# Early loads, casts and PE order of a fused linear-attention and ELU feed-forward kernel, arranged anew

## The chip, the cores and the metric

The kernel runs on one core of one Trainium2 chip. A time is the device time of one execution in microseconds (us). Five engines work side by side, each through its own queue of instructions: PE (TensorE: matmuls and transposes; its weight loads are shown as PEld), DVE (VectorE), ACT (ScalarE), POOL (GpSimd) and SP (SyncE, which here only issues DMAs). POOL issues the loads of the weights and of most q, k and v.

## The reference

```
def _attn_ref(q, k, v):                 # each 8 batches x 8 heads x 576 x 64
    q_s = softmax(q, axis=-1)           # over the 64 elements of a head
    k_s = softmax(k, axis=2)            # over the 576 positions
    kv = np.einsum('bhsd,bhse->bhde', k_s, v)
    return np.einsum('bhsd,bhde->bhse', q_s, kv)

def _moe_ref(x, w_in, w_out):           # x: 4608 x 512, w_in: 512 x 2048, w_out: 2048 x 512
    h = x @ w_in
    g = np.where(h > 0.0, h, np.exp(np.minimum(h, 0.0)) - 1.0)
    return g @ w_out

def reference(...):
    x = attn_out.transpose(0, 2, 1, 3).reshape(B * S, H * D)
    return _moe_ref(x, w_in, w_out)
```

The two softmax calls stand here for the lines that subtract the maximum, take the exponential and divide by the sum.

## The kernel before, in words

**Attention.** The work is cut into 16 units (`n`), two for each batch. For a unit, ACT takes the exponentials of q and k (L395 or, in two parts, L419; L399), DVE sums q over the head (L421), inverts (L423), and DVE or POOL multiplies (L433, the result is `QS`). Units 0 and 1 do q in two parts of 5 and 4 chunks. `v` is cast to bf16 (`VB`, a copy by `copy`, L277). PE transposes `QS` (L457, copied out as `qsT`), forms k^T v (L507), DVE divides it by the sums of k into `MBLK` (L516, L520), and PE multiplies `qsT` with `MBLK` (L550 for the first two units, L538 later). The result is copied (L277) into `XT`, which holds x transposed.

**Feed-forward.** The 4608 tokens are 9 blocks of 512 (`j`). For each block there are 8 groups (`g`) of 256 columns of d_ff. A group is 8 matmuls of 512 columns of `XT` with `W1` (L620, in `hg_mm`), then ELU: exp on ACT (L646), and either ACT's relu (L648) with DVE's L652, or DVE's L657 and L659. The result is `GR`. For blocks 0 and 1 the second product with `W2` is direct (L673, in `out_mm`): 4 token slices by 16 row tiles `jj`, 64 matmuls for a block. From block 2 on it goes in pairs of blocks with sums of halves (L733, L757, L806).

**Block 0 is special.** The products of its groups 0 to 2 with `W1` go by `kc`, the four quarters of d_model, as units 0 and 1 and W1's quarters arrive; groups 3 to 7 come whole, in the order 3, 4, 5, 7, 6. The second product of block 0 goes by quarters of `W2` (`jj` 0 to 3, 4 to 7, 8 to 11, 12 to 15), and among its matmuls stand the transposes, k^T v and L538 of units 2 and 3, which block 1 needs.

**Loads.** SP issues q, k and v of units 0 and 1. POOL issues everything else that the first 50 us need, in this order: W1 for groups 0 to 2 in four pieces by `kc` (384 KB each, the first held back until k0 has landed), W1 for groups 3, 4 and 5 (512 KB each), W1 for groups 6 and 7 (1 MB), and then the quarters of W2 (1 MB each) and q, k, v of units 2 and 3 (576 KB each). `load_w1` (L377), `load_w2` (L385) and `load` (L359) record these.

**Order.** Each operation is recorded by `S.add` with the engines that may do it, its cost, and what it reads and writes; it gets a number. The strings of `ORDER` give each engine's numbers in a fixed order (found beforehand by a solver), and which engine does an operation that several could do follows from the string that it stands in. `AFTER` holds extra pairs (a waits for b). Spare matmuls (L892) fill PE until the first real work. `emit` issues the instructions with their semaphores.

Of the kernel before, what the change touches and what calls it, by code (L numbers as in the profile page):

```python
# [11 lines left out]
B, H, S, D = 8, 8, 576, 64  # L12
# [37 lines left out]
    "act": (  # L50
# [12 lines left out]
    "dve": (  # L63
# [37 lines left out]
}  # L101

AFTER = ((208, 196), (227, 255), (234, 268), (300, 281))


class Op:
    __slots__ = ("eng", "dur", "emit", "deps", "key", "idx", "start", "end",
                 "dma", "sem", "val", "clock", "nbytes", "side", "early", "alts")

# [165 lines left out]
class Gen:  # L275
# [586 lines left out]
    def program(self):  # L862
# [4 lines left out]
        for n, t in ((0, "q"), (1, "q"), (0, "k"), (0, "v"), (1, "k"), (1, "v")):  # L867
            self.load(n, t, -40, "sp")
            if (n, t) == (0, "k"):
                gate = S.ops[-1]  # L870
# [219 lines left out]
```

## Time and profile before

| | us |
|---|---|
| median of 3 runs | 291.89 |
| lowest and highest run | 291.81, 292.03 |
| profiled execution: span from its first to its last instruction | 290.4 |
| PE busy | 280.6 (97%) |
| DVE, ACT, POOL busy | 225.5, 209.7, 167.8 |
| first matmul with W1 (L620) | 14.20 |
| first matmul with W2 (L673) | 29.68 |
| first matmul of block 1 with W1 | 48.28 |
| first matmul of block 2 with W1 | 70.94 |

The profile is of one execution and gives its span, counted from the first to the last instruction; the runs are timed from outside, and the profile holds no outside time of that execution itself. The median is 1.5 us above the span. Times of rows are counted from the start of the span. A row of the timeline merges neighbouring instructions of one kind: its start, its length, and xcount of them.

### The profile page before, as it was taken

How to read it: one execution, taken by the hardware profiler on the slowest of the kernel's cores; microseconds unless marked ns; L12 is line 12 of the kernel's file. 1: busy time of each engine (PE TensorE's matmuls, PEld its weight loads, DVE VectorE, ACT ScalarE, POOL GpSimd, SP SyncE). 2: the span in 40 equal slices, each digit the busy share in tenths (PEclk: the TensorE clock that was granted, in tenths of full speed). 3: DMA queues.
4: the chain of work that ended last, by engine and by line, in shares of the span. 5: the costliest groups of instructions: out<-in, count | busy, mean ns of one | idle time of the engine just before them, and what ended most of it. 6: DMA issues, size and time to landing. Idle time of an engine off the chain costs nothing.

```text
span 290.4 us, 5465 instructions
## 1 busy us (share of the span) xinstructions
PE 280.6 (97%) x2176; PEld 243.7 (84%) x2176; DVE 225.5 (78%) x425; ACT 209.7 (72%) x237; POOL 167.8 (58%) x161
## 2 busy tenths in 40 slices
PE   2899999999999999999999999999999999999995
PEld 0488787778888899989999988989999999988995
DVE  3758834777699978989996987688977786794884
ACT  4857839989899899968995598975385656665510
POOL 1991335523869778676574886757314234277741
PEclk9999999999999999999999999999999999999999
DMA  7999999798896838739939295313102002300334
GB/s 259 399 363 390 389 389 339 163 260 323 238 349 163 241 91 228 202 78 305 178 96 222 56 292 129 76 40 71 46 18 56 0 2 67 78 2 1 92 73 128
DMA packets 36474, 50.04 MB, mean 172 GB/s; under 512 B 16352, under 2 KB 18144, under 8 KB 36448
## 3 DMA queue, kind: packets, MB, share of 16 engines
q1 hardware_dynamic: 29680, 33.96, 43.7%
q0 software_dynamic: 6528, 15.47, 17.8%
q8 instruction: 17, 0.28, 0.5%
q10 hardware_dynamic: 240, 0.26, 0.3%
q14 instruction: 9, 0.07, 0.1%
HBM read 36.70 MB, written 9.44 MB: 159 GB/s over the span
## 4 chain that ended last, share of the span: by engine, by line
PE 94%; DMA 2%; POOL 2%; SPq 0%; issue 0%; DVE 0%
PE PS L620 46%; PE PS L806 32%; PE PS L673 10%; PE PS L538 3%; DMA KR<-in_k_dram 2%; PE PS L507 2%; POOL W L377 1%; POOL VB L277 0%; PE PS L457 0%; POOL QS L433 0%; SPq L359 0%; PE PS L550 0%; DVE OSB L815 0%
## 5 line engine op out<-in xcount | busy, mean ns | idle before, releaser
L620 PE MATMUL PS<-XT,W 128*128 128x512 f32 x576 | 142.0, 393 | 0.1
L620 PEld LDWEIGHTS PS<-XT,W 128*128 128x128 f32 x576 | 105.0, 188 | 21.2 <-DVE GR L659 0.5
L652 DVE SCALAR_TENSOR_TENSOR GR<-PS,GE 128x512 fp32r<-128x512 f32 x112 | 76.8, 686 | 18.7 <-ACT GE L648 16.7
L646 ACT ACTIVATE GE<-PS 128x1024 f32<-128x1024 f32 x56 | 57.4, 1025 | 40.0 <-PE PS L620 34.2
L757 POOL TENSOR_TENSOR GR<-GR 128x256 fp32r<-128x256 f32 (+1 forms) x48 | 47.2, 996 | 31.5 <-DVE SB L757 16.6
L648 ACT ACTIVATE GE<-GE 128x1024 f32<-128x1024 f32 x56 | 59.4, 1061 | 1.4
L806 PE MATMUL PS<-W,GR 128*128 128x256 f32 x336 | 53.7, 283 | 0.0
L806 PE MATMUL PS<-TB,GR 128*128 128x256 f32 x336 | 51.3, 283 | 0.0
L806 PEld LDWEIGHTS PS<-W,GR 128*128 128x128 f32 x336 | 47.6, 191 | 1.7
L806 PEld LDWEIGHTS PS<-TB,GR 128*128 128x128 f32 x336 | 45.7, 191 | 0.7
L433 POOL TENSOR_TENSOR QS<-QR,RZQ 128x1152 f16<-128x1152 f32 (+1 forms) x16 | 30.4, 1898 | 21.4 <-DVE RZQ L423 19.7
L815 DVE TENSOR_TENSOR OSB<-OSB,PS 128x256 f32<-128x256 f32 x84 | 34.7, 416 | 10.3 <-PE PS L806 9.2
L673 PE MATMUL PS<-W,GR 128*128 128x512 f32 x128 | 32.7, 396 | 0.0
L757 POOL TENSOR_TENSOR GR<-SB,GR 128x256 fp32r<-128x256 f32 (+1 forms) x18 | 17.3, 971 | 24.6 <-PE PS L806 12.7
L673 PEld LDWEIGHTS PS<-W,GR 128*128 128x128 f32 x128 | 23.3, 188 | 5.0 <-DMA W<-in_moe_w_out_dram 0.5
L757 POOL TENSOR_TENSOR SB<-GR 128x256 fp32r<-128x256 f32 (+1 forms) x20 | 19.2, 965 | 13.7 <-DVE GR L652 6.4
L421 DVE TENSOR_REDUCE ZQ<-QR 128x18 f32<-128x1152 f32 (+2 forms) x18 | 21.7, 1207 | 6.1 <-ACT QR L419 4.8
L757 DVE TENSOR_TENSOR GR<-GR 128x256 fp32r<-128x256 f32 (+1 forms) x36 | 21.3, 603 | 0.6 <-PE PS L806 0.6
L277 POOL CAST VB<-VR 128x1152 bf16<-128x1152 f32 (+1 forms) x11 | 11.9, 1084 | 13.1 <-DMA VR<-in_v_dram 13.1
L646 ACT ACTIVATE ESB<-PS 128x1024 f32<-128x1024 f32 x16 | 16.1, 1024 | 4.5 <-PE PS L620 3.4
L399 ACT ACTIVATE KR<-KR 128x1152 bf16<-128x1152 f32 x16 | 18.4, 1155 | 0.8 <-DMA KR<-in_k_dram 0.8
L277 ACT ACTIVATE XT<-PS 128x512 fp32r<-128x512 f32 (+6 forms) x23 | 13.6, 595 | 6.3 <-PE PS L538 3.2
(58 smaller groups left out, 271.4 us busy)
## 6 DMA issues: line engine op xcount, KB each, us to landing
out_dram<-OSB SPq DMA_DIRECT2D x61, 128.0 KB, 2.4
QR<-in_q_dram SPq DMA_DIRECT2D x12, 576.0 KB, 4.9
KR<-in_k_dram SPq DMA_DIRECT2D x12, 576.0 KB, 6.3
VR<-in_v_dram SPq DMA_DIRECT2D x12, 576.0 KB, 5.1
W<-in_moe_w_out_dram POOLq DMA_DIRECT2D x4, 1024.0 KB, 16.7
QR<-in_q_dram POOLq DMA_DIRECT2D x4, 576.0 KB, 12.1
VR<-in_v_dram POOLq DMA_DIRECT2D x4, 576.0 KB, 13.0
KR<-in_k_dram POOLq DMA_DIRECT2D x4, 576.0 KB, 11.1
```

Of the source, the lines that this page charges most:

```text
L277: return e.activation(dst, src, AF.Copy) if e is self.nc.scalar else e.tensor_copy(dst, src)
L399: S.add("act", t_act(1152, False), lambda e: e.activation(ek[:, :, :, :].rearrange("p h c d -> p (h c d)"), flat(k), AF.Exp), key - 2, X=[ ...
L421: S.add("dve", t_dve(m), lambda e, qp=qp, zp=zp: e.tensor_reduce(zp, qp, AX.X, ALU.add), key - 3, R=[f"qR{i}{x}" for x in xs], W=[f"ZQ{i}{ ...
L433: lambda e, qp=q[:, :, a:b, :], rz=rz, dst=qs[:, :, a:b, :]: e.tensor_tensor(dst, qp, rz, ALU.mult),
L620: last = e.matmul(P[:, t * 512:(t + 1) * 512], self.W1[:, kc, tt * 128:(tt + 1) * 128], self.XT[:, kc, rc:rc + BLK], start=(kc == 0), stop ...
L646: S.add("act", t_act(1024, True), lambda e: e.activation(ge, P, AF.Exp), key, W=own, X=banks)
L648: S.add("act", t_act(1024, False), lambda e: e.activation(ge, ge, AF.Relu, bias=1.0, scale=-1.0), key, X=own)
L652: S.add("dve", t_dve(512 if j else 1024), lambda e, u=u: e.scalar_tensor_tensor(*(x[:, :, u, :] if j else x for x in (gt, P)), 0.0, ge[:, ...
L673: last = e.matmul(dst, self.tile(jb, jj, ts), self.W2[:, jj, c0:c1], start=(jj == 0), stop=(jj == 15))
L757: lambda e: e.tensor_tensor(dst, a, b, op), key, R=R, W=W, X=X, after=after)
L806: last = e.matmul(dst, a[i][:, y_, :], b[i][:, y_, :], start=start and i == 0 and y_ == 0, stop=stop and i == len(grps) - 1 and y_ == z - ...
L815: S.add("dve", t_dve(256), lambda e: e.tensor_tensor(dst, a, b, ALU.add), key, R=R, W=W, X=X, after=after)
```

## The change

- **W1.** The three transfers for groups 3, 4 and 5 become one of 1.5 MB (rows of 3 KB in place of 1 KB). The first quarter (`kc` 0) of groups 0 to 2 comes in two pieces, group 0 (128 KB) and groups 1 and 2 (256 KB). POOL issues `kc` 3 first, then groups 1 and 2 of `kc` 0, group 0 of it, `kc` 1, `kc` 2, groups 3 to 5.
- **The gate.** These first five transfers wait for the exponential of k0 on ACT (operation 21), by five pairs in `AFTER`; before, the first waited for the landing of k0.
- **The queue after that.** q2, W1 groups 6 and 7, W2's first and second quarter, v2, k2, q3, W2's third quarter, k3, v3, and W2's last quarter in two halves of 512 KB. Before: W1 groups 6 and 7, W2's first quarter, q2, the second quarter, q3, v2, k2, the third and the last quarter, k3, v3.
- **The product with W2's last quarter** (block 0) goes in pieces of two matmuls in place of four.
- **Engines.** The `VB` casts of units 0 and 1 (640 and 512 elements each) go to DVE (before: ACT 640, POOL 512). The products L433 of units 0, 2 and 3 swap: POOL takes the 5 chunks, DVE the 4; unit 1's are both on DVE. Unit 2's cast goes from POOL to ACT, the copy of its transposes from ACT to DVE. Of block 0's four output copies, DVE does two in place of none. Unit 3's transposes and L538 use the PSUM tile `AB` in place of `C`.
- **PE's order.** The 13 spare matmuls (13 rather than 12, in groups of 8, 1, 3, 1) stand elsewhere; among the L673 pieces the side work of units 2 and 3 stands at other places (unit 3's k^T v ahead of the whole last quarter, its two L538 with one piece or more between them); the two halves of block 1's group 1 stand ahead of the last two pieces of block 0's second product. From about 75 us on, all orders are the same but for the numbers, which are 4 higher.

```diff
@@ ORDER, first rows
     "pe": (
-        "35 52 33 37 56 57 54 60 80 78 79 64 65 82 81 84 87 85 88 83 86 89 99 103 110 133 121 107 "
-        "147 148 155 156 149 125 150 158 157 127 153 168 145 171 169 151 176 175 170 177 159 178 "
-        "172 165 192 194 191 193 253 259 258 257 265 211 264 266 272 220 270 271 277 279 283 222 "
+        "34 32 51 36 53 55 59 56 79 78 63 64 81 82 84 87 85 88 80 83 86 89 99 103 110 133 121 107 "
+        "148 147 156 155 125 149 157 127 150 158 145 168 151 170 153 171 169 159 177 175 178 165 "
+        "176 179 172 180 196 198 181 182 195 197 257 263 261 268 262 269 215 270 276 275 274 281 "
...
     "gp": (
-        "1 32 14 15 24 16 17 18 48 40 19 20 21 69 68 70 73 72 71 74 75 76 77 120 131 116 143 163 "
+        "1 27 18 15 14 16 17 19 67 20 68 69 71 70 72 73 74 75 76 77 119 131 142 139 163 144 132 "
...
-AFTER = ((208, 196), (227, 255), (234, 268), (300, 281))
+AFTER = ((212, 200), (231, 259), (238, 272), (304, 285), (14, 21), (15, 21), (16, 21), (17, 21), (18, 21))
...
-    def load_w2(self, s, key, after=()):
+    def load_w2(self, jj0, jj1, key):
         w = self.w_out.rearrange("(jj p) c -> p jj c", p=128)
-        sl = slice(s * 4, (s + 1) * 4)
+        sl = slice(jj0, jj1)
         self.S.add("gp", ISSUE["gp"], lambda e: e.dma_start(self.W2[:, sl, :], w[:, sl, :]), key,
-                   W=[f"W2_{s}"], dma=f"w2{s}", nbytes=1 << 20, after=after)
+                   W=[f"W2_{s}" for s in range(jj0 // 2, jj1 // 2)], dma=f"w2{jj0}", nbytes=jj1 - jj0 << 18)
...
-            if (n, t) == (0, "k"):
-                gate = S.ops[-1]
-        self.load_w1(0, 3, (0,), -30, [gate])
+        self.load_w1(0, 1, (0,), -30)
+        self.load_w1(1, 3, (0,), -30)
         for kc in range(1, 4):
             self.load_w1(0, 3, (kc,), -30)
-        for g0, g1 in ((3, 4), (4, 5), (5, 6), (6, 8)):
+        for g0, g1 in ((3, 6), (6, 8)):
             self.load_w1(g0, g1, range(4), -30)
...
         self.load(2, "q", -28)
-        self.load_w2(0, -29)
-        self.load_w2(1, -29)
+        self.load_w2(0, 4, -29)
+        self.load_w2(4, 8, -29)
         for n, t in ((2, "k"), (2, "v"), (3, "q")):
             self.load(n, t, -28)
-        self.load_w2(2, -27)
-        self.load_w2(3, -25)
+        self.load_w2(8, 12, -27)
         for t in "kv":
             self.load(3, t, -26)
+        for jj in (12, 14):
+            self.load_w2(jj, jj + 2, -25)
...
         for jq in range(4):
             for ts in range(4):
-                self.out_mm(0, ts, (ts + 2) % 4, 4 * jq, 4 * jq + 4, key)
+                for jj in range(4 * jq, 4 * jq + 4, 2 if jq == 3 else 4):
+                    self.out_mm(0, ts, (ts + 2) % 4, jj, jj + (2 if jq == 3 else 4), key)
```

In PE's row, numbers 147 to 158 and 168 to 171 are pieces of the product with W2's first three quarters, 175 to 182 (175 to 178 before) those with the last one, 99, 103, 110, 133 and 121 block 0's groups 3, 4, 5, 7 and 6, 159 unit 3's k^T v, and 192 and 194 before, 196 and 198 after, the two halves of block 1's group 1. In POOL's row, 14 to 21 are W1, 67 to 77 the queue after that, 116 and 120 before and 119 and 142 after casts or products.

More of the change, by code (lines that the diff above doesn't have):

```diff
@@ L408, in stage1 @@
                 cost = {"act": t_act(int(576 * (h1 - h0)), False), "gp": 77 + 488 * (h1 - h0)}
+                if vconv == "pair":
+                    cost["dve"] = t_dve(576 * h1, 2)
                 S.add(dict(sorted(cost.items(), key=lambda x: x[0] == "act" and vconv != "pair" or x[0] == "gp" and h0 == 5)),
@@ L678, in out_mm @@
                      for x in ((0, 1) if jb == 0 else (tp,))), []) +
-                [f"W2_{s}" for s in range(jj0 // 4, (jj1 + 3) // 4)], X=[f"b{bk}"])
+                [f"W2_{s}" for s in range(jj0 // 2, (jj1 + 1) // 2)], X=[f"b{bk}"])
     def out_store(self, jb, ts, bk, key):
@@ L718, in w2 @@
         z0, z1 = GROUPS[grp]
-        return [f"W2_{s}" for s in range(z0 // 2, (z1 + 1) // 2)]
+        return [f"W2_{s}" for s in range(z0, z1)]
     def combos(self, key, grp):
@@ L866, in program @@
         self.init()
-        for n, t in ((0, "q"), (1, "q"), (0, "k"), (0, "v"), (1, "k"), (1, "v")):
+        for n, t in ((0, "q"), (0, "k"), (0, "v"), (1, "q"), (1, "k"), (1, "v")):
             self.load(n, t, -40, "sp")
-            if (n, t) == (0, "k"):
-                gate = S.ops[-1]
-        self.load_w1(0, 3, (0,), -30, [gate])
+        self.load_w1(0, 1, (0,), -30)
+        self.load_w1(1, 3, (0,), -30)
         for kc in range(1, 4):
             self.load_w1(0, 3, (kc,), -30)
-        for g0, g1 in ((3, 4), (4, 5), (5, 6), (6, 8)):
+        for g0, g1 in ((3, 6), (6, 8)):
             self.load_w1(g0, g1, range(4), -30)
@@ L885, in program @@
         self.side(0, -3, self.kv_mm(1, 0))
-        kv1 = S.ops[-1]
+        S.spare_until = S.ops[-1]
         self.m(1, 0, -12)
-        S.spare_until = S.ops[-4]
         self.ao_parts(1, 0, -2)
@@ L917, in ao @@
         def ao(n, x, kvn=()):
-            ps, eng = (C if x == 0 else AB, "both") if n == 3 else (AB, "act")
+            ps, eng = AB, "both" if n == 3 else "act"
             def go():
@@ L945, in wide @@
             if n < BYDMA:
-                return n, lambda: self.tp(n, C if n == 3 else AB, due(n) - 4, ("act",))
+                return n, lambda: self.tp(n, AB, due(n) - 4, ("act",))
             return n, lambda: self.widen(n, due(n))
```

130 rows, old and new, of the table ORDER are left out of this document.

## The prediction

> **What bounds the kernel now.** I read the page first (busy times, then the chain), then the windows by stage, then what TensorE (PE) waited for.
>
> ```profile
> span 290.4 us, 5465 instructions
> PE 280.6 (97%) x2176; PEld 243.7 (84%) x2176; DVE 225.5 (78%) x425; ACT 209.7 (72%) x237; POOL 167.8 (58%) x161
> ...
> PE 94%; DMA 2%; POOL 2%; SPq 0%; issue 0%; DVE 0%
> ```
>
> PE is 97% busy and 94% of the chain. The rest of the chain lies at the head. The profiled execution spans 290.4; the median of the runs is 291.89, 1.5 us more, which lies outside the first and last instruction. I leave those 1.5 us as they are, so a difference of the spans is a difference of the times. 0.2% is 0.58 us, about what a measurement of this kernel can tell from no change: faster means below 291.31, slower above 292.47.
>
> ```profile
> 10.00:14.00 4.00, 3.20 (x76) 1.70 (x78) 2.39 (x7) 4.00 (x7) 4.00 (x7) 1.00 1.16 401
> 14.00:20.00 6.00, 6.00 (x61) 4.96 (x46) 2.53 (x6) 2.42 (x4) 6.00 (x9) 1.00 1.66 362
> 20.00:30.00 10.00, 10.00 (x48) 8.34 (x47) 8.53 (x9) 8.26 (x9) 3.23 (x5) 1.00 1.34 388
> 75.00:290.00 215.00, 212.04 (x1657) 191.46 (x1655) 177.61 (x345) 152.46 (x170) 130.87 (x117) 1.00 0.46 120
> ```
>
> These are the windows (length, then PE, PEld, DVE, ACT, POOL busy, granted clock, DMA share, GB/s). From 14 us on PE has nothing but work, at a granted clock of 1.00, and the DMA runs at full rate beside it: 401, 362 and 388 GB/s. The 362 are the stretch in which W1's groups 3, 4 and 5 come as three transfers. After 75 us the order of every engine is unchanged, PE is full, and DMA needs 120 GB/s. So a shift of PE at 75 us is carried to the end, and only the first 75 us have to be worked out. The waits of PE's weight loads there, and PE's rows:
>
> ```profile
> PEld PS L620 <- DVE GR L659: 0.5, 1, 0.5
> PEld PS L673 <- DMA W<-in_moe_w_out_dram: 0.5, 1, 0.5
> PEld PS L620 <- DVE GR L652: 0.5, 1, 0.5
> ...
> PEld PS L538 <- DVE MBLK L520: 0.2, 1, 0.2
> PEld PS L673 <- DVE GR L659: 0.2, 1, 0.2
> ```
>
> ```profile
> 14.20 1.66 PE L620 MATMUL PS<-XT,W 128*128 128x512 f32 x6
> ...
> 16.16 13.32 PE L620 MATMUL PS<-XT,W 128*128 128x512 f32 x58
> ...
> 29.68 5.18 PE L673 MATMUL PS<-W,GR 128*128 128x512 f32 x20
> ...
> 46.64 1.20 PE L673 MATMUL PS<-W,GR 128*128 128x512 f32 x4
> 47.68 0.76 PE L538 MATMUL PS<-qsT,MBLK 128*128 128x256 f32 x4
> ```
>
> ```profile
> 48.28 7.88 PE L620 MATMUL PS<-XT,W 128*128 128x512 f32 x32
> 56.00 1.55 PE L673 MATMUL PS<-W,GR 128*128 128x512 f32 x6
> ...
> 58.18 0.73 PE L673 MATMUL PS<-W,GR 128*128 128x512 f32 x2
> 58.95 3.91 PE L620 MATMUL PS<-XT,W 128*128 128x512 f32 x16
> ```
>
> And from the chain of waits, in order of time:
>
> ```profile
> 16.32 13.16 PE PS L620 x58
> ...
> 31.80 3.06 PE PS L673 x12
> ...
> 54.05 2.11 PE PS L620 x8
> ```
>
> A 512-column matmul takes 13.16/58 = 0.227. Weight loads run ahead, so the loss is not their wait but the gap between a row's start plus its matmuls and the next start. Five losses:
> - (a) W2's second quarter: 29.68 + 8 x 0.227 = 31.50, next start 31.80: 0.30.
> - (b) unit 3's MBLK: 46.64 + 0.91 = 47.55 against 47.68: 0.13.
> - (c) block 1's fourth group, behind VectorE's (DVE) L652: 48.28 + 24 x 0.227 = 53.73 against 54.05: 0.32.
> - (d) block 1's first L673, behind L659: 54.05 + 1.82 = 55.87 against 56.00: 0.13.
> - (e) its fifth group, behind L659: 58.18 + 0.45 = 58.63 against 58.95: 0.32.
>
> Together 1.20 us. That is what the change can win behind the head.
>
> **Part by part: the head.**
>
> ```profile
> L377 POOL DMA_DIRECT2D W<-in_moe_w_in_dram x8: 576/727/862, 8.1 to 15.1; - x8
> ...
> DMA to landing us min/median/max: 5.1/5.6/9.7
> ```
>
> ```profile
> 8.14 1.34 POOL L377 DMA_DIRECT2D W<-in_moe_w_in_dram  x2 [0.60 <-DMA KR<-in_k_dram]
> 9.39 0.87 POOL L277 CAST VB<-VR 128x512 bf16<-128x512 f32 x1
> ...
> 13.00 0.73 POOL L277 CAST VB<-VR 128x512 bf16<-128x512 f32 x1
> ```
>
> ```profile
> 7.86 1.16 ACT L399 ACTIVATE KR<-KR 128x1152 bf16<-128x1152 f32 x1 [0.78 <-DMA KR<-in_k_dram]
> ...
> 12.77 0.74 ACT L277 ACTIVATE VB<-VR 128x640 bf16<-128x640 f32 x1
> ```
>
> ```profile
> 19.24 0.78 DVE L657 TENSOR_SCALAR ESB<-ESB 128x1024 f32<-128x1024 f32 x1 [2.19 <-ACT ESB L646]
> L657 DVE TENSOR_SCALAR ESB<-ESB x8: 682/689/780, 19.2 to 67.5; 128x1024 f32<-128x1024 f32 x8
> ```
>
> *Gate.* The first W1 transfer was issued at 8.14, when k0 had landed. It now waits for the exponential of k0, which ends at 7.86 + 1.16 = 9.02, so it is issued near 9.3, 1.2 later. Behind it on POOL's queue stand all the other bulk transfers. POOL loses its two casts (0.87 and 0.73) between them, so the five W1 issues behind the gate end near 9.3 + 5 x 0.73 = 13.0, and the queue is back in step. Its first piece landed at 8.1 + 5.1 = 13.2, yet DMA moved 401 GB/s in 10 to 14 us, with the first units' k and v ahead of it. I take the landing as set by bytes: still 13.3. The other end is 9.3 + 5.1 = 14.4.
>
> *Casts.* The values of units 0 and 1 are cast on DVE, 1152 elements in two instructions. The nearest row, another single-source pass from SBUF to SBUF, does 1024 in 0.68 to 0.78, so 0.8 to 0.9 for both. Before, unit 1's casts ended at 13.00 + 0.73 = 13.73 on POOL and 12.77 + 0.74 = 13.51 on ACT; on DVE from about 12.4 they would end near 13.3. That is 0.4 earlier, but W1's group 1, the second piece, lands only near 14.0 (13.3 and 256 KB at 0.4 MB per us). First matmul with W1: 14.1, against 14.20.
>
> *One transfer for groups 3 to 5.* Before, group 3 started 18 matmuls into the row of 16.16, at 20.24, that is 6.04 after the first. Now PE is there at 14.1 + 6.0 = 20.1. The first four pieces (1.57 MB) are in at 13.3 + 3 x 0.393/0.40 = 16.2; another 1.57 MB at 388 GB/s take 4.05, so 20.3, and PE starts near 20.4: **+0.15**. Three small transfers let PE start on the first third; one large one does not. Ends: no wait at all (-0.1), or the 362 GB/s of that stretch, 4.35 us and 20.6 (+0.4).
>
> *Groups 6 and 7* now come behind q2: 20.3 + (0.59 + 1.05)/0.388 = 24.5, needed at 20.4 + 24 x 0.227 = 25.8. Before, they landed at 15.1 + 9.7 = 24.8, although the bytes alone give 16.2 + 4.35 + 2.7 = 23.3. These 1.5 us are unexplained; if they recur, 26.0, +0.2.
>
> **Part by part: block 0's second product (29.7 to 48.3).**
>
> ```profile
> L385 POOL DMA_DIRECT2D W<-in_moe_w_out_dram x1: 797/797/797, 17.3 to 17.3; - x1
> ...
> DMA to landing us min/median/max: 14.5/14.5/14.5
> ```
>
> ```profile
> L359 POOL DMA_DIRECT2D VR<-in_v_dram x1: 856/856/856, 22.4 to 22.4; - x1
> ...
> DMA to landing us min/median/max: 22.3/22.3/22.3
> ```
>
> These are single transfers picked out by window: W2's second quarter landed at 17.3 + 14.5 = 31.8, v3 at 22.4 + 22.3 = 44.7. The bytes ahead of W2's second quarter are the same as before, but W1's groups come 0.3 faster, so 31.5; PE needs it at 29.68 + 0.15 + 1.82 = 31.65. **(a) goes: -0.30**, or -0.15 if the landing stays at 31.8.
>
> k3 and v3 pass W2's last quarter (1.05 MB, 2.7 us): v3 lands near 41.7, and the two halves of the quarter near 43.1 and 44.4. PE leaves this stage near 48.28 - 0.43 + 0.25 = 48.1 in work of the old order; take off the last quarter's 16 matmuls (3.63) and unit 3's L538 (0.6), and the last quarter starts at 43.9 and wants its second half two pieces (0.91) later, at 44.8. Both halves are there, by 0.8 and 0.4. Three pieces now stand between unit 3's k^T v and its L538, in place of one: **(b) goes: -0.13**. Without that cover it would stay.
>
> *What is added.* Unit 3's product with 1/z is shared anew: POOL takes 5 chunks, DVE 4, both released by the same reciprocal, and the transposes of unit 3 wait for POOL.
>
> ```profile
> L433 DVE TENSOR_TENSOR QS<-QR,RZQ x4: 818/822/959, 8.2 to 37.1; 128x640 f16<-128x640 f32 x4
> 12.01 1.17 POOL L433 TENSOR_TENSOR QS<-QR,RZQ 128x512 f16<-128x512 f32 x1
> ```
>
> POOL's 640 elements take 1.17 x 640/512 = 1.46, against 0.82 to 0.96 on DVE: 0.5 later, of which most is hidden by the L673 piece placed before the transposes (0.91). I take **+0.1**, ends 0 and +0.4. Splitting L673 into two-matmul pieces adds no instruction for PE.
>
> **Part by part: block 1 (48 to 75).** Two halves of group 1's product with W1 now stand ahead of the last two L673 pieces. Between the end of group 1 and the start of group 3, which takes its banks, PE has 4 matmuls more, 0.91. The wait (c) of 0.32 is less than that: **-0.32**. The chain exp, relu, L652 starts as much earlier, so (d) goes too: **-0.13**. (e) hangs on DVE's next group, and there the gain is shared with DVE's own queue: I take half, **-0.16**, ends 0 and -0.32.
>
> **Sum.** Gains 0.30 + 0.13 + 0.32 + 0.13 + 0.16 = 1.04. Costs 0.15 + 0.1, and 0.1 more for DVE's casts beside POOL's issues (0.78 against 0.68 in the row of L657, the slow one beside an issue). Net -0.69: 291.89 - 0.69 = **291.2**. With the ends of the terms 290.9 to 291.6.
>
> **Rivals.**
>
> *The port.* DVE's casts meet POOL's W1 issues from 9.4 to 13 us. The row says 0.1 for such a meeting. If the casts ran at one element per cycle (0.82 for 640 in the row of L433), both would take 1.5 instead of 0.85: first matmul at 14.7, group 3 at 20.75, so +0.5 in place of +0.15: 291.55; with one issue (0.73) waited out on top, 292.2. The Trainium skill, SBUF — State Buffer, "Who interferes with whom", says that a cast in DVE's two-port mode and GpSimd, writing of DMA descriptors included, fully block one another for the whole instruction. By that rule a cast would wait out an issue, which is the upper time; the trace's 0.1 speaks against a full block, though no run here shows a cast of this kind. Chance 0.22.
>
> *The queue lags.* The unexplained 1.5 us come again, at groups 6 and 7 and then at W2's second quarter: +0.2 and +0.15, perhaps +0.1 at unit 3: 291.6 to 291.7. For it: it happened before, in the same stretch. Chance 0.18.
>
> *Slower: the gate is carried through.* If DMA has nothing to move while POOL waits, the first piece lands at 14.4, group 3's transfer at 16.2 + 1.1 + 4.35 = 21.65, and PE stands until 21.7: +1.5 in place of +0.15, all later loads as late, so nothing is won back: 291.2 + 1.35 = 292.55. It decides once the first W1 piece lands after about 14.3. Against it: 401 GB/s from 10 to 14 us with k1 and v1 still to land. Chance 0.12.
>
> *The forecast* has 0.48: its core lies just below 291.31.
>
> **Chances.** Faster by over 0.2%: 0.40 from the forecast and 0.05 from the milder port and lag cases, 0.45. Within 0.2%: 0.40, from the rest of these. Slower: 0.15, the gate and the port's far end. Range 290.8 to 292.4: it takes in the terms' ends and both middle rivals, and leaves out the far side of the gate.
>
> **What would show it.** In the profile after: first L620 at 14.1; PE idle for a few tenths before group 3 at about 20.4, put down to W1's transfer; no wait of L673 for W2 near 31.8; k3 exponentiated near 40 and v3 cast near 41.7 rather than 43 and 44.7; the waits of L620 for L652 near 54 gone; block 2's first matmul some 0.7 earlier. Wrong would be: a first L620 after 14.5, a new wait of PE for W2's last halves near 44, or transposes of unit 3 waiting half a us for POOL.

## The result and the profile after

The changed kernel takes 295.52 us (median of 4 runs, 295.04 to 295.77), the kernel before 291.96 (4 runs, 291.81 to 292.45): a ratio of 1.0115, 95% interval 1.0098 to 1.0132. It is 3.6 us slower, where 0.7 us faster was forecast. The profiled execution took 295.77 with a span of 294.0.

The page, first lines and the chain by engine:

```profile
span 294.0 us, 5467 instructions
PE 281.8 (96%) x2177; PEld 244.0 (83%) x2177; DVE 232.2 (79%) x433; ACT 207.4 (71%) x232; POOL 167.1 (57%) x158
...
PE 88%; DMA 6%; DVE 2%; ACT 1%; POOL 1%; SPq 0%; issue 0%
```

DMA has gone from 2% of the chain to 6%, and DVE and ACT stand in it. The windows (length; PE, PEld, DVE, ACT, POOL; clock, DMA share, GB/s), two of the kernel before and then three of the changed one:

```profile
14.00:18.00 4.00, 4.00 (x53) 3.29 (x38) 1.77 (x5) 0.60 (x2) 4.00 (x6) 1.00 1.57 368
18.00:24.00 6.00, 6.00 (x28) 4.99 (x27) 4.69 (x5) 5.50 (x6) 5.22 (x8) 1.00 1.54 374
```

```profile
10.00:14.00 4.00, 3.10 (x52) 1.52 (x50) 3.85 (x10) 3.44 (x5) 4.00 (x8) 1.00 1.09 343
14.00:18.00 4.00, 3.06 (x46) 2.18 (x47) 2.32 (x6) 1.20 (x2) 4.00 (x7) 1.00 1.06 280
18.00:24.00 6.00, 4.46 (x20) 3.24 (x19) 3.34 (x3) 4.03 (x4) 4.53 (x7) 1.00 1.17 406
```

From 10 to 18 us DMA moves 343 and 280 GB/s where it moved 401 and 368, and PE stands idle for 0.9 of 4 us and 1.5 of 6. The granted clock is 1.00. The timeline of POOL's W1 issues and of PE after the change:

```profile
9.72 4.01 POOL L377 DMA_DIRECT2D W<-in_moe_w_in_dram  x6 [1.40 <-ACT KR L399]
```

```profile
15.11 1.16 PE L622 MATMUL PS<-XT,W 128*128 128x512 f32 x4
...
17.34 4.92 PE L622 MATMUL PS<-XT,W 128*128 128x512 f32 x20 [0.61 <-DMA W<-in_moe_w_in_dram]
23.79 9.37 PE L622 MATMUL PS<-XT,W 128*128 128x512 f32 x40 [1.53 <-DMA W<-in_moe_w_in_dram]
33.00 0.53 PE L540 MATMUL PS<-qsT,MBLK 128*128 128x64 f32 x4
...
37.12 0.68 PE L459 MATMUL PS<-ID,QS 128*128 128x128 f16 x9
37.90 2.11 PE L675 MATMUL PS<-W,GR 128*128 128x512 f32 x8
...
54.01 5.60 PE L622 MATMUL PS<-XT,W 128*128 128x512 f32 x24
59.45 1.98 PE L675 MATMUL PS<-W,GR 128*128 128x512 f32 x8
61.35 0.78 PE L509 MATMUL PS<-VB,KR 64*64 64x65 bf16 x72
62.13 3.92 PE L622 MATMUL PS<-XT,W 128*128 128x512 f32 x16
...
74.46 2.02 PE L622 MATMUL PS<-XT,W 128*128 128x512 f32 x8
```

The whole loss stands ahead of group 3:

| stage | before | after | difference |
|---|---|---|---|
| start to block 0's group 3 | 20.24 | 23.79 | +3.55 |
| group 3 to block 2's first matmul | 70.94 - 20.24 = 50.70 | 74.46 - 23.79 = 50.67 | -0.03 |
| from there to the end of the span | 219.5 | 219.5 | 0 |

The first W1 matmul is 0.91 late (15.11). At 17.34, where W1's `kc` 1 ends a wait, 20 matmuls are left to group 3; before, that was at 20.24 - 20 x 0.227 = 15.70, so another 0.7 is lost. And 17.34 + 20 x 0.227 = 21.88, but PE goes on at 23.79, when the one transfer for groups 3 to 5 is in: 1.9 more. Of the 0.91, some 0.4 is not the change's: SP's last load, v1, landed at 12.71 in this execution and at 12.34 in that of the kernel before, although it was issued earlier here (3.35 against 3.58).

### The profile page after: what moved, and what is told of

It reads as the page before. It is cut to its first block, busy times and chain, and to the rows that moved or that the text cites. A ratio compares the mean times of both kernels' runs of the same rounds, so it can differ in the third digit from the quotient of the medians.

```text
span 294.0 us, 5467 instructions
## 1 busy us (share of the span) xinstructions
PE 281.8 (96%) x2177; PEld 244.0 (83%) x2177; DVE 232.2 (79%) x433; ACT 207.4 (71%) x232; POOL 167.1 (57%) x158
## 3 DMA queue, kind: packets, MB, share of 16 engines
HBM read 36.70 MB, written 9.44 MB: 157 GB/s over the span
## 4 chain that ended last, share of the span: by engine, by line
PE 88%; DMA 6%; DVE 2%; ACT 1%; POOL 1%; SPq 0%; issue 0%
PE PS L622 42%; PE PS L808 32%; PE PS L675 9%; DMA W<-in_moe_w_in_dram 4%; PE PS L540 3%; DMA KR<-in_k_dram 2%; PE PS L509 2%; POOL W L377 1%; DVE QS L435 1%; DVE ZQ L423 0%; DVE GR L654 0%; ACT KR L399 0%; DVE GR L661 0%; ACT ESB L650 0%; ACT ESB L648 0%; SPq L359 0%
## 5 line engine op out<-in xcount | busy, mean ns | idle before, releaser
L622 PE MATMUL PS<-XT,W 128*128 128x512 f32 x576 | 142.4, 394 | 2.2 <-DMA W<-in_moe_w_in_dram 2.1
L622 PEld LDWEIGHTS PS<-XT,W 128*128 128x128 f32 x576 | 104.8, 188 | 23.9 <-DMA W<-in_moe_w_in_dram 3.2
L435 POOL TENSOR_TENSOR QS<-QR,RZQ 128x1152 f16<-128x1152 f32 (+1 forms) x15 | 30.6, 2042 | 33.6 <-DVE RZQ L425 33.6
L675 PE MATMUL PS<-W,GR 128*128 128x512 f32 x128 | 32.9, 395 | 0.1
L675 PEld LDWEIGHTS PS<-W,GR 128*128 128x128 f32 x128 | 23.4, 188 | 4.7 <-DVE GR L661 0.3
L648 ACT ACTIVATE ESB<-PS 128x1024 f32<-128x1024 f32 x16 | 16.2, 1027 | 9.0 <-PE PS L622 8.6
L277 ACT ACTIVATE XT<-PS 128x512 fp32r<-128x512 f32 (+5 forms) x23 | 13.9, 606 | 10.4 <-PE PS L540 7.1
L277 ACT ACTIVATE OSB<-PS 128x256 f32<-128x256 f32 (+1 forms) x21 | 7.9, 386 | 13.6 <-PE PS L808 13.6
```

The source lines that it names most:

```text
L277: return e.activation(dst, src, AF.Copy) if e is self.nc.scalar else e.tensor_copy(dst, src)
L435: lambda e, qp=q[:, :, a:b, :], rz=rz, dst=qs[:, :, a:b, :]: e.tensor_tensor(dst, qp, rz, ALU.mult),
L622: last = e.matmul(P[:, t * 512:(t + 1) * 512], self.W1[:, kc, tt * 128:(tt + 1) * 128], self.XT[:, kc, rc:rc + BLK], start=(kc == 0), stop ...
L648: S.add("act", t_act(1024, True), lambda e: e.activation(ge, P, AF.Exp), key, W=own, X=banks)
L675: last = e.matmul(dst, self.tile(jb, jj, ts), self.W2[:, jj, c0:c1], start=(jj == 0), stop=(jj == 15))
```

## The experiments

Three theories for the head were on record: A, the one large transfer; B, DVE's casts in the way of POOL's descriptors; C, the late gate. In the experiments' kernels line numbers are 5 lower, so L617 is the changed kernel's L622, and L372 is L377. A ratio is to runs of the kernel before made beside that experiment; their median was 292.05 for e1 to e4, 292.22 for e5 to e8 and 291.96 for e9 to e12, so experiments of different sets are compared by their ratios.

**e1_three**

```diff
-        for g0, g1 in ((3, 6), (6, 8)):
+        for g0, g1 in ((3, 4), (4, 5), (5, 6), (6, 8)):
```

> The changed kernel, but W1's groups 3, 4 and 5 come as three transfers of 512 KB again (all else as changed). Theory A, the one large transfer is the cost: the DMA that ran at 280 GB/s from 14 to 18 us comes back to about 390, PE starts group 3 near 20.5 in place of 23.79, and the time falls from 295.5 to about 291.5 to 292. Theory B, DVE's casts hold up the writing of descriptors on POOL, and theory C, the late gate lets the DMA queue run empty: the slow stretch from 13 to 17 us stays, group 3 starts near 21 on its own third, but groups 6 and 7 still land near 28, so the time falls by 1.2 at most, to about 294.3.

294.47 (292.84 to 294.65), ratio 1.0070 (1.0047 to 1.0093). It falls by 1.05, as B and C had it: 14 to 18 us still run at 291 GB/s, and PE reaches group 3 earlier (22.30 in place of 23.79) only because its own third is there.

**e2_casts** (DVE's string without 22, 23, 39, 38)

```diff
 "act": ... 33 +22 52 35 37 +38 57 ...
 "gp":  1 27 18 +23 15 14 16 17 +39 19 67 ...
```

> The changed kernel, but the VB casts of units 0 and 1 go to ACT (640 elements) and POOL (512) again, POOL's between W1's issues (all else as changed). Theory B (DVE's casts in the way of POOL's descriptors): no slow stretch, 390 GB/s from 14 to 18 us, the large W1 transfer lands near 20.4 in place of 23.75, and the time is about 291.5. Theories A and C: the transfer still lands near 23.5 to 24, and the time stays at 295 to 296.

295.84 (295.39 to 297.93), ratio 1.0149 (1.0107 to 1.0191). 14 to 18 us run at 245 GB/s, so DMA is slow without DVE's casts too. By itself this run does not clear them, since POOL's own cast now stands between W1's issues (the second at 10.86, 10.43 in the changed kernel). The next run does: it keeps DVE's casts, and DMA is fast. With both, B falls as the cause of the slow DMA.

**e3_gate**

```diff
-AFTER = (..., (14, 21), (15, 21), (16, 21), (17, 21), (18, 21))
+AFTER = (..., (14, 9), (15, 9), (16, 9), (17, 9), (18, 9))
```

> The changed kernel, but the first W1 transfers wait for the landing of k0 again and not for its exponential (all else as changed). Theory C (the gate lets the queue run empty): W1's first issue moves from 9.72 to about 8.4, the slow stretch from 13 to 17 us goes, the large transfer lands near 20.4, and the time is about 291.4. Theories A and B: still a slow stretch, the large transfer lands near 23 to 23.8, and the time stays at 295 to 295.5.

293.52 (292.80 to 293.85), ratio 1.0048 (1.0031 to 1.0065). This one edit gives back 2.0 us, though not all that C had named (291.4). POOL's timeline, the windows, PE's timeline and one of its waits:

```profile
8.61 3.91 POOL L372 DMA_DIRECT2D W<-in_moe_w_in_dram  x6 [0.18 <-issue]
```

```profile
10.00:14.00 4.00, 2.90 (x53) 1.37 (x51) 3.92 (x10) 3.43 (x6) 4.00 (x7) 1.00 1.20 395
14.00:18.00 4.00, 3.69 (x50) 3.00 (x51) 2.29 (x6) 1.22 (x3) 4.00 (x6) 1.00 1.25 400
```

```profile
15.08 1.17 PE L617 MATMUL PS<-XT,W 128*128 128x512 f32 x4
...
16.55 13.77 PE L617 MATMUL PS<-XT,W 128*128 128x512 f32 x60
```

```profile
PEld PS L504 <- DVE VB L272: 1.0, 1, 1.0
```

W1's issues stand 1.1 earlier, DMA runs at 395 and 400 GB/s, and PE goes through 60 matmuls without a wait: the one large transfer landed at 20.73, and PE came to group 3 at 16.55 + 20 x 0.227 = 21.09. C holds. The large transfer costs nothing here, but only because PE came late: at 20.24, where group 3 stood in the kernel before, PE would have waited 0.5 for it. What is left of the head's loss is the first W1 matmul at 15.08. It stands behind unit 1's k^T v, which waits for DVE's casts, and these wait for v1, which landed at 12.82 in this profile.

**e4_head** (e1, e2 and e3 together, and W1's kc 0 in one piece and first)

```diff
 "gp": 1 28 14 15 24 16 17 18 40 19 20 68 21 ...     (14 to 21 are W1, 24 and 40 casts, 68 is q2)
```

> The changed kernel with its whole head undone: W1's kc 0 in one piece and first, groups 3 to 5 in three transfers, the gate at the landing of k0, the casts on ACT and POOL. The order behind the head, the queue of W2, k3 and v3, and L433's halves stay as changed. If all of the loss lies in the head and the rest is worth what the prediction said (1.04 gained, 0.1 lost), then the time is about 291.0, and no matmul waits for W1. If the loss lies behind the head as well, it is above 292.

292.94 (292.77 to 293.28), ratio 1.0026 (1.0016 to 1.0037). The first W1 matmul is at 14.62, group 3 at 20.54, so this head is within 0.3 of the old one. But block 2 starts at 71.73, 51.19 after group 3, where before took 50.70: the part behind the head gains nothing, and the loss there was to be found next (e6, e7). The stretch is not a fixed length: the changed kernel and the other runs with its orders there (e1, e2, e3, e10, e11, e12) took 50.65 to 51.23.

**e5_before_gate** (the kernel before with its AFTER and one pair more)

```diff
-AFTER = ((208, 196), (227, 255), (234, 268), (300, 281))
+AFTER = ((208, 196), (227, 255), (234, 268), (300, 281), (14, 22))
```

> The kernel before with one pair more in AFTER: its first W1 transfer waits for the exponential of k0 too, as in the changed kernel. Nothing else is changed: four pieces of 384 KB, three of 512 KB, casts on ACT and POOL. Theory C (the late first issue alone makes the DMA slow from 13 to 17 us): the first issue moves from 8.14 to about 9.4, DMA falls below 330 GB/s in 14 to 18 us, W1's second to fourth piece and the groups 3 to 5 land 1 to 2 us later, PE waits for W1, and the time is 293.5 to 294.5. Theory D (it takes the split pieces or the large transfer as well): the landings move by 0.5 at most, and the time is 291.9 to 292.4.

293.11 (292.65 to 294.18), ratio 1.0035 (1.0022 to 1.0049), between the two ranges named. Its windows and PE's first rows:

```profile
10.00:14.00 4.00, 3.34 (x51) 1.61 (x50) 1.69 (x6) 4.00 (x7) 4.00 (x7) 1.00 1.12 366
14.00:18.00 4.00, 3.71 (x53) 2.60 (x52) 2.22 (x6) 0.81 (x2) 4.00 (x7) 1.00 1.06 305
```

```profile
15.68 1.66 PE L615 MATMUL PS<-XT,W 128*128 128x512 f32 x6
```

The gate alone, with the old pieces, makes DMA slow again (305 in place of 368). Beside its own runs of the kernel before it costs 1.0 us (0.35%), not the 3.4 (1.15%) of the changed kernel. In this profile the whole of it falls on the first matmul (15.68 against 14.20), because POOL's product and cast stand behind W1's issues, and the cast ends only at 15.21. From there to group 3 (21.74) it takes 6.06, as before (6.04): W1 comes in pieces that PE can begin with, so PE loses nothing by the slow DMA.

**e6_dve_order and e7_widen_act** (edits of e4_head, whose numbers are one higher)

```diff
 e6 "dve": -119 124 121 125 +119 124 125 121          (121 the product, 125 the group's max)
 e7 "gp":  -213 215 232 +213 232     "act": 265 266 +215 302
```

> The kernel of e4_head with one exchange in DVE's order: group 6's max (L659 of the kernel before) ahead of unit 2's product with 1/z, which no longer meets POOL's half of the same product. Theory E (DVE's product with two SBUF inputs is held until POOL's is done): the product takes 0.67 in place of 1.75, the group's max ends about 1.1 earlier, PE has 0.2 to 0.4 less idle time near 34 us, and the time falls from 292.94 to about 292.6. Rival: the 1.75 are hidden, and the time stays at 292.9.

> The kernel of e4_head, but unit 4's widening copy of qsT goes back from POOL to ACT, behind block 1's fourth relu. Theory E (DVE's min-and-add in its two-port mode is held while POOL's copy runs): it takes 0.69 in place of 1.28, block 1's fifth group starts 0.5 to 0.6 earlier, and the time falls to about 292.4. Rival: ACT is the later one there (its exponentials then stand behind the copy), the wait only changes its name, and the time stays within 0.2 of 292.9.

e6: 292.71 (292.32 to 293.96), ratio 1.0024 (1.0012 to 1.0037). e7: 292.61 (292.48 to 293.01), ratio 1.0012 (1.0003 to 1.0021). The timelines of e4_head, DVE's and then POOL's, at 31 and at 57 us:

```profile
31.80 1.76 DVE L430 TENSOR_TENSOR QS<-QR,RZQ 128x512 f16<-128x512 f32 x1
...
56.97 1.28 DVE L654 TENSOR_SCALAR ESB<-ESB 128x1024 f32<-128x1024 f32 x1 [1.09 <-ACT ESB L643]
```

```profile
31.21 1.80 POOL L430 TENSOR_TENSOR QS<-QR,RZQ 128x640 f16<-128x640 f32 x1 [7.42 <-DVE RZQ L420]
...
56.56 1.15 POOL L272 CAST qsT<-QT 128x1152 fp32r<-128x1152 f16 x1
```

The first DVE instruction in e6, the second in e7:

```profile
33.18 0.68 DVE L430 TENSOR_TENSOR QS<-QR,RZQ 128x512 f16<-128x512 f32 x1
```

```profile
57.36 0.69 DVE L654 TENSOR_SCALAR ESB<-ESB 128x1024 f32<-128x1024 f32 x1 [1.09 <-ACT ESB L643]
```

DVE's product takes 1.76 when POOL's half of it began first, 0.68 once that has ended; the min-and-add 1.28 beside POOL's copy, 0.69 without it. In both, DVE's instruction ends 0.55 after POOL's does (33.01 and 33.56; 57.71 and 58.25), though the two had stood side by side for 1.21 in one case and 0.74 in the other; the product in the changed kernel, e3 and e7 has the same 0.55. An instruction that was only slowed would not end at a fixed distance: it is held until POOL's is done, and then most of its own 0.68 is still to come. Theory E holds. PE sees it: e4_head's fifth group of block 1 starts at 59.56 with 0.59 idle behind DVE, e7's at 59.36 with none, although e7's group 3 came 0.6 later. From group 3 to block 2 the two take 50.70 and 50.55, in place of 51.19. The times do not show it: the ratios of e4, e6 and e7 are 1.0026, 1.0024 and 1.0012, with intervals that overlap. So the two collisions are shown in the traces, and what each is worth in the kernel's time is not.

The changed kernel itself has the first of the two alone. There POOL's copy comes after the min-and-add:

```profile
57.08 0.70 DVE L659 TENSOR_SCALAR ESB<-ESB 128x1024 f32<-128x1024 f32 x1
59.03 1.15 POOL L277 CAST qsT<-QT 128x1152 fp32r<-128x1152 f16 x1
```

**e8_both** (e6 and e7, and W1's groups 6 and 7 ahead of q2)

> The kernel of e4_head with both of these edits, and with W1's groups 6 and 7 ahead of q2 again. If the three losses add up (0.3, 0.5 and 0.15): 292.0, level with the kernel before. If the order of PE behind the head is worth the 1.0 that the prediction gave it, 291.3 or less.

292.41 (292.19 to 293.68), ratio 1.0009 (0.9999 to 1.0019): not told from the kernel before, which ran at 292.22 beside it. That is the first case (level), and not the 291.3 of the second. Unit 5's cast on POOL (56.25 to 57.40) now met the same min-and-add, which took 1.17.

**e9_old_head** (e8 with the old orders up to group 3)

```diff
 "gp": 1 32 14 15 24 16 17 18 48 40 19 20 21 68 ...   (32 and 48: products back on POOL)
```

> The kernel of e8_both with the head's orders of the kernel before on all engines (unit 0's and 1's products with 1/z on the engines they had, the same order of PE and of the spare matmuls up to block 0's third group). Behind the head it is e8_both: k3 and v3 ahead of W2's last quarter, that quarter in halves, block 1's group 1 ahead of the last pieces of block 0. From group 3 to block 2's first matmul e8_both took 50.5 us against 50.7 before, e7_widen_act 50.55 against 50.7. If the head is as before (group 3 at 20.24): 0.2 faster than the kernel before, about 291.7 to 291.9 beside 292.0 to 292.2. If the head's orders were not the cause of the later group 3 (20.5 to 21.1 in e4 to e8): 292.4, as e8_both.

292.18 (291.75 to 293.78), ratio 1.0005 (0.9993 to 1.0018): level. In its profile, from group 3 at 16.50 + 18 x 0.227 = 20.58:

```profile
16.50 13.32 PE L617 MATMUL PS<-XT,W 128*128 128x512 f32 x58
...
70.78 2.00 PE L617 MATMUL PS<-XT,W 128*128 128x512 f32 x8
```

50.20 to block 2, 0.5 less than before, so in this profile the part behind the head does win once the collisions are away. The head did not come back to 20.24 in this profile, but v1 landed 0.47 later in it (12.81 against 12.34): counted from v1, the first W1 matmul comes after 1.76 here (14.57) and after 1.86 in the kernel before. No version beat the kernel before beyond its interval.

**e10_later_gate**

```diff
-(14, 21), (15, 21), (16, 21), (17, 21), (18, 21)
+(14, 44), (15, 44), (16, 44), (17, 44), (18, 44)
```

> The changed kernel with the gate one operation of ACT later: the first W1 transfers wait for the exponential of q1's second part, so the first issue moves from 9.72 to about 10.3. Theory C (what counts is how far POOL's queue has been filled when SP's loads end at 12.7): the slow stretch lasts longer, the large transfer lands 1 to 1.7 us later than the 23.75 of the changed kernel, and the time is 296.3 to 297.3. If the delay is only passed on (1 for 1): 24.3 and 296.1. If the slow stretch has nothing to do with the issue: 295.5.

295.35 (294.65 to 296.05), ratio 1.0118 (1.0094 to 1.0142). As a step it failed: in its profile the first issue stood at 9.72 again, since k0 itself came half a us earlier. It still says something on how the loss grows. With k0 all of SP's loads came earlier; v1 landed at 12.21, only 2.5 after the first issue. 14 to 18 us ran at 271 GB/s, slow as in the changed kernel, and yet the large transfer landed at 22.25, before the 23.75 there. The four runs took 294.65, 294.69, 296.02 and 296.05. So in the profiled run, the fastest of the four, a shorter lead of POOL did not make the loss larger, and the loss differs by 1.4 us from run to run.

**e11_q2_on_sp**

```diff
-        self.load(2, "q", -28)
+        self.load(2, "q", -28, "sp")
 "sp": 8 11 9 10 12 13 +67 ...      "gp": ... 17 19 -67 20 ...
```

> The changed kernel, late gate and all, but q2 is issued by SP behind v1 and not by POOL behind the large W1 transfer: DMA has SP's 576 KB to move while POOL's queue fills. Theory C (POOL's transfers run slowly where DMA takes them up as they are written): 14 to 18 us at 370 GB/s or more in place of 280, the large transfer lands near 22 although 576 KB more go ahead of it, and the time is about 293.7 to 294.3. Rival (W1's small pieces or a disturbed memory are slow by themselves): the stretch stays slow, the large transfer lands at 24.5 or later, and the time is 296 or more.

294.64 (293.93 to 294.99), ratio 1.0083 (1.0064 to 1.0101). POOL's timeline, the windows and PE's timeline:

```profile
10.06 4.81 POOL L372 DMA_DIRECT2D W<-in_moe_w_in_dram  x7 [1.71 <-ACT KR L394]
```

```profile
10.00:14.00 4.00, 2.65 (x49) 1.11 (x46) 3.79 (x10) 3.37 (x6) 3.94 (x7) 1.00 1.10 395
14.00:18.00 4.00, 2.61 (x44) 1.96 (x45) 1.99 (x5) 1.04 (x3) 4.00 (x8) 1.00 1.27 396
```

```profile
22.95 9.38 PE L617 MATMUL PS<-XT,W 128*128 128x512 f32 x40 [0.41 <-DMA W<-in_moe_w_in_dram]
```

W1 is issued even later than in the changed kernel (10.06), and yet DMA runs at 395 and 396 GB/s, and the large transfer is in 0.8 earlier although 576 KB more went ahead of it. So it is not the hour of the issue by itself. The run agrees with theory C: POOL's transfers run slowly when SP's loads end before POOL's queue is well filled. In the changed kernel v1 landed 3.0 after the first W1 issue; in e3_gate, and in the kernel before, 4.2; here q2 4.5. The time misses its range by 0.3, since W1's first pieces came behind q2 (first W1 matmul at 16.31).

**e12_gate_casts** (e3 and e2 together)

> The changed kernel with two edits undone, the gate (back at k0's landing) and the casts of units 0 and 1 (back on ACT and POOL). The one large W1 transfer stays. In e3_gate the first W1 matmul stood at 15.1 behind DVE's casts (1.47 for the two of unit 1, beside POOL's issues), and group 3 came at 21.08, after the large transfer at 20.73. If the casts are the rest of the head's loss: first matmul near 14.6, group 3 at 20.7, bound by the transfer, and 293.1 in place of 293.52. If ACT and POOL are as late as DVE: 293.5.

294.68 (293.51 to 297.05), ratio 1.0097 (1.0059 to 1.0135): a miss. With POOL's casts between W1's issues the second W1 issue stood at 10.11 and the large one at 13.45, 14 to 18 us ran at 348 GB/s, and PE waited at 21.97 for the large transfer. The first W1 matmul did come at 14.91 in place of 15.08, but v1 had landed 0.6 earlier (12.21 against 12.82), so counted from v1 it came later. The cost of the casts can't be had from this run. Nor does the step from e3 to e4 show it (21.09 to 20.54 at group 3, ratios 1.0048 and 1.0026 with overlapping intervals): v1 landed 0.6 earlier in e4's profile too.

**The queue in all these runs.** e12 and e4_head have the same first issue (8.35) and the same landing of v1 (12.21), but in e12 POOL's cast moved the second issue from 9.05 to 10.11. So the first issue alone does not decide. What does sort the runs is how much of W1 POOL had finished issuing when SP's last load (v1, in e11 q2) landed:

| issued by then | runs | GB/s, 14 to 18 us |
|---|---|---|
| 768 KB | e2, e10 | 245, 271 |
| 1152 KB | changed kernel, e1, e5, e12 | 280, 291, 305, 348 |
| 2048 KB | kernel before, e4, e6 to e9 | 368 to 372 |
| 3072 KB | e11, e3 | 396, 400 |

The runs at 2048 KB have W1's groups 3 to 5 in three transfers, as e1 and e5 have. No run varies this amount by itself, so it is an order that the runs show, and not yet a cause.

## Why the prediction was wrong

**The step that failed** is the gate. I took the landing as "set by bytes", because 401 GB/s were moved from 10 to 14 us. The first piece landed at 13.65, near that and well below the 14.3 at which the rival was to decide. But the bytes behind it did not follow: `kc` 1 was in at 17.30 and the last of the first pieces at 18.29 (16.2 forecast), groups 3 to 5 at 23.75 (20.3). The row of 401 GB/s showed what DMA moves with a filled queue, and the change took the filling away. The rival "the gate is carried through" had the right place and sign, chance 0.12, but the wrong form: a delay of 1.1 passed on, 292.55, where a slow stretch of 4 us followed. e3 and e11 show it; the gate is 2.0 of the 3.6 us.

**The large transfer** was priced at 0.15, with 0.4 as its far end. That was too little even with the queue filled: in e3 it landed at 20.73 where 20.3 was forecast, and PE at the forecast 20.1 would have waited 0.6. It cost nothing there only because PE came at 21.09, which is luck. Beside the slow queue it makes PE wait for the last byte, and e1 gives 1.05 back.

**The casts.** I priced both at 0.8 to 0.9; the rows of DVE's casts of unit 0 and of unit 1, two instructions each:

```profile
9.75 0.94 DVE L277 CAST VB<-VR 128x640 bf16<-128x640 f32 x2
...
12.80 1.48 DVE L277 CAST VB<-VR 128x512 bf16<-128x512 f32 x2
```

0.94 and 1.48, the second 0.6 above my price, with 0.1 put down for the meeting with POOL's issues. k^T v of unit 1 waited for it, and the first W1 matmul stood at 15.1, not 14.1. But the longer casts are the smaller part of that. Five profiles, by where the casts are done and in which order PE works:

| kernel | casts, PE's order | v1 landed | unit 1's casts ended | first W1 matmul | after v1 |
|---|---|---|---|---|---|
| before | ACT and POOL, old | 12.34 | 13.73 | 14.20 | 1.86 |
| changed | DVE, new | 12.71 | 14.28 | 15.11 | 2.40 |
| e3_gate | DVE, new | 12.82 | 14.25 | 15.08 | 2.26 |
| e4_head | ACT and POOL, new | 12.21 | 13.81 | 14.62 | 2.41 |
| e9_old_head | ACT and POOL, old | 12.81 | 14.08 | 14.57 | 1.76 |

I had v1 at the hour of the old profile; it came 0.37 later. From v1, the casts end 1.57 later on DVE and 1.39 later before, which is 0.2. The rest, some 0.35, is PE's new order, which I did not price: a matmul of L552, which stood ahead of unit 1's k^T v in the kernel before, now stands between it and the first W1 matmul (14.33, 14.75, 15.11; before 13.79, then 14.20). With the casts back on ACT and POOL it is still 2.41 (e4); with the old order it is 1.76 (e9, which also puts the products of units 0 and 1 back).

**The port rival** stood at 0.22, and I let the trace's 0.1 speak against a full block. For POOL's own arithmetic the Trainium skill (SBUF — State Buffer, "Who interferes with whom") was right: full holds, 1.76 for 0.68 and 1.28 for 0.69. For the writing of descriptors no full block shows: unit 0's casts took 0.94 beside two issues of 0.71 and 0.63, unit 1's 1.48 beside issues of 1.21 and 1.17, half as much again and not a whole issue more. Why the second pair was longer is not shown. My row was of this second kind, a meeting with an issue, and I used it for the first: the new halves of L435 were priced at +0.1 for POOL's length alone, though both start at the same reciprocal. In the changed kernel:

```profile
34.96 1.75 DVE L435 TENSOR_TENSOR QS<-QR,RZQ 128x512 f16<-128x512 f32 x1
```

It delays group 6's max, and PE goes from the transposes at 37.12 to L675 at 37.90, 0.78 where the same step took 0.49 before (34.70 to 35.19). The move of unit 4's copy from ACT to POOL, which the list of the change leaves out, I had not priced at all; in the changed kernel it met nothing (59.03), in e3, e4 and e6 it met the min-and-add.

**Block 1.** (c), (d) and (e) came as forecast or better: 54.01 + 24 x 0.227 = 59.46, and the next row starts at 59.45; behind it no wait up to 62.13. The three waits that are gone made 0.77, where 0.61 was put down. But a new one stands behind them, at 67.78:

```profile
PEld PS L622 <- DVE GR L661: 0.3, 1, 0.3
```

```profile
67.25 0.51 PE L540 MATMUL PS<-qsT,MBLK 128*128 128x384 f32 x2
67.78 2.12 PE L622 MATMUL PS<-XT,W 128*128 128x512 f32 x8
```

From the fifth group to block 2 PE took 74.46 - 62.13 = 12.33, against 70.94 - 58.95 = 11.99. So block 1 as a whole gained only 0.36: 74.46 - 51.25 = 23.21, less 0.91 for the four matmuls moved into it, against 22.66.

**Block 0's second product.** (a) is gone, but (b) was never a wait of PE:

```profile
39.04 1.20 PE L673 MATMUL PS<-W,GR 128*128 128x512 f32 x4
40.08 0.46 PE L538 MATMUL PS<-qsT,MBLK 128*128 128x320 f32 x2
```

These rows of the kernel before have the same 1.04 for four matmuls behind transposes as (b) has behind k^T v, with no wait named. In both, the second of the four starts 0.34 after the first and the others follow at 0.23: coming back to L673 from smaller matmuls costs up to 0.13. The changed order comes back more often (nine runs of L675 up to block 1's first matmul and one behind it, six before), and the product from its first matmul to block 1's first takes 51.25 - 33.36 = 17.89 for 60 matmuls and the side work, against 18.60 for 64: 0.2 more, not 0.43 less. With 0.13 lost between group 3 and this product (9.57 against 9.44), 0.2 in it and 0.36 won in block 1, the 0.94 forecast from group 3 to block 2 (1.04 less 0.1) came out at 0.03. With the collisions away, e9's profile has 0.5 of it.

**Open.** Why POOL's transfers run at 245 to 305 GB/s for some 4 us when they are taken up soon after they are written is not shown; e2 and e3 rule out DVE's casts, no more. The traces tell that it is not every packet (a piece that a DMA engine moves at once): of those of 3 KB from 14 to 18 us, the median took 136 ns in the changed kernel and 156 in e3, but the longest 2.18 us against 0.18. Open too are how the loss grows with the delay (e10 and e12 speak against the first issue alone), and what DVE's casts and the collisions are worth in the kernel's time.

## What to carry to other kernels

A gate ahead of a queue of loads must not be judged by when its first transfer lands: look for how far that queue is filled when the other queue runs dry, and read the rate behind it. Where two profiles are laid side by side, count from an event that the change does not touch (here v1's landing) before a difference of a few tenths is given to the change. A merged transfer is free only while its last byte comes before its first user, so price it with the queue slow as well. In both pairs met here, a product or a min-and-add of DVE beside a product or a copy of POOL, the two ran one after the other: where one event releases both, put another of DVE's instructions between them.

## What the hardware showed unexpectedly

- POOL's queue, first issue 3.0 us before the other queue ends: 280 GB/s for 4 us (245 to 305 in e1, e2, e5); 4.2 us before: 395 to 400 in e3 with pieces of the same shape. The same lead of 3.9 gave 348 (e12) with 1152 KB of W1 issued when that queue ended, and 368 (e4) with 2048 KB.
- DVE's min-and-add is held by POOL's copy until that ends: 1.28 against 0.69; its product by POOL's product: 1.76 against 0.68.
- The load of k0, issued at 1.75 in the kernel before as in the changed one, let its exponential start at 7.86 in one and at 8.25 in the other. In the 14 profiles it landed between 7.69 and 8.56, and v1 moved with it. A head bound by it moves by some tenths of a us from one execution to the next, more than several of the terms above. The row after the change (the other stands in the prediction):

```profile
8.25 1.16 ACT L399 ACTIVATE KR<-KR 128x1152 bf16<-128x1152 f32 x1 [1.39 <-DMA KR<-in_k_dram]
```
